# Second addition of signs issued behind the next thresholds on GpSimd, in a fused top-32 attention and mixture-of-experts kernel

## The chip, the cores and the metric

One NeuronCore of a Trainium2 chip runs the whole program. The metric is the device time of one execution in microseconds (us); the number before is the median of three executions.

## What is computed

Attention over 8 batches and 8 heads, 576 tokens, head size 64, where each query keeps only its 32 largest scores; then a layer of 8 experts, of which each token uses the one with the largest gate.

```python
scores = scale * np.matmul(q, k.transpose(0, 1, 3, 2))
kth = np.partition(scores, -top_k, axis=-1)[..., -top_k:-top_k + 1]
mask = scores >= kth                       # top_k = 32
scores = np.where(mask, scores, -1000000000.0)
attn = softmax(scores); attn_out = np.matmul(attn, v)
...
expert_idx = np.argmax(x @ w_gate, axis=1)
h = np.maximum(x[mask] @ w1[e], 0.0); out[mask] = gate_w[mask, None] * (h @ w2[e])
```

(`softmax` stands for the reference's shift, exponential and division.)

## The kernel before, in words

The attention is worked off in 144 groups. A group is two blocks of 128 query rows, each with its 576 scores, so one tile of 128 x 2 x 576 numbers, called `sb` in the profile (seven of them rotate). What happens to group g, by function, line and engine:

- `scores` and `scores_left` (L371, L389): TensorE multiplies into PSUM (tiles `ps`, `px`), ScalarE copies to `sb` (L386, L406), and SyncE issues the DMA that keeps the raw scores in DRAM (`sc`, L423).
- `topk` (L434): VectorE finds the 32nd largest score of every row. Its list `one` has 24 MAX8 instructions over pieces of 48 scores (L1079), `two` merges them (L1086), and `three_`, five instructions, ends it: one reduction of L450, two reductions of L1082 on VectorE, and two small GpSimd instructions of L1082 that make the thresholds, tile `nb`. `three_` is kept in `delayed` and issued in the next step, between that step's MAX8 instructions.
- `softmax(g, us, i)` (L488), once for each of the two blocks i: ScalarE compares the scores with the threshold (activation Sign with `nb` as its bias, L494) and writes signs to the tile `sg` of that block (there is one `sg` for i = 0 and one for i = 1, written in every step); GpSimd adds the signs into the scores in place (L495). The signs are coded so that scores under the threshold vanish in the exponential.
- `transp` (L497): TensorE transposes the masked scores into PSUM (`tt`, nine instructions, L501); `exps` (L503): ScalarE exponentiates them (L505); `av` (L508): TensorE multiplies with the values (`px`, L515).

The order is written out by hand: no scheduler moves instructions, and each engine executes its own list in the order of the Python calls. The main loop (L1059) does, in step t, in this order: `exps` of group t-4, `softmax` of group t-2 for block 0, what jobs have left for TensorE, `scores` of group t+3, `softmax` of t-2 for block 1, `av` of t-5, `scores_left` of t+3, `transp` of t-3, ScalarE's part of jobs; then the 24 MAX8 of group t with the `delayed` thresholds of group t-1 between the first nine of them, then `two` of group t (with one small GpSimd instruction, tile `nbt`) and VectorE's part of jobs; then the jobs' GpSimd part. Jobs are pieces of other work (`advance`, L944): preparing q and k, sums and scaled output rows of finished heads (tiles `sums`, `xm`, `lp`), the repair of rows with ties (`r_...`), and routing of tokens to experts (`table`). So the thresholds that `softmax` of group t-1 will need in step t+1 are computed by VectorE early in step t, and GpSimd finishes them in step t behind both additions of group t-2.

After the last group the expert layer runs: TensorE multiplies by the experts' weights (L1264, L1279), which are split into two parts (L1009 to L1012).

Of the kernel before, what the change touches and what calls it, by code (L numbers as in the profile page):

```python
# [14 lines left out]
OP = mybir.AluOpType  # L15
# [15 lines left out]
LAG = 2  # L31
# [24 lines left out]
def attention_moe(ctx, tc, q, k, v, w_gate, w1, w2, out):  # L56
    nc = tc.nc
# [121 lines left out]
    SG = []  # L179
    for i in range(2):  # L180
        t = consts.tile([128, S], BF, name=f"sg{i}")
# [3 lines left out]
    def upper(t):  # L185
        return t.bitcast(I8).rearrange("p (n b) -> p n b", b=2)[:, :, 1]
# [25 lines left out]
    for b in range(2):  # L212
        for p in range(HP):
            for h in range(2):
# [4 lines left out]
                a = attr[:, t0:t0 + 2 * MAIN - 1:2, :]  # L219
# [4 lines left out]
                a = attr[h * LEFT:(h + 1) * LEFT, tl_, :]  # L224
# [8 lines left out]
    for i in range(3):  # L233
        t = work.tile([128, 2, KW], F32, name=f"qk{i}", bufs=1)
# [30 lines left out]
    for i in range(NV):  # L265
        t = jobs.tile([128, 2, VW], F32, name=f"rv{i}", bufs=1)
# [4 lines left out]
    VV, SB, EX, ET, XT, SCD, SCP = {}, {}, [], {}, {}, {}, {}  # L271
# [22 lines left out]
    def flush(queue):  # L294
        while queue:
            queue.pop(0)()

    def load_v(n):
        b, hf = divmod(n, H // 4)
        rv = VV[n] = VB[n % NV]  # L300
        VV.pop(n - NV, None)
        w = MAIN * D
        for g in range(2):
            hs = slice(4 * hf + 2 * g, 4 * hf + 2 * g + 2)
            both = bass.AP(rv.tensor, rv[:, g].offset, [list(rv.ap[0]), [w + 4 * D, 2], [1, w]])
            nc.sync.dma_start(both, v[b, hs, 0:M, :].rearrange("h (p i) d -> p h (i d)", p=128))
            for i in range(2):
                o = w + (1 - i) * D
                nc.sync.dma_start(rv[i * LEFT:(i + 1) * LEFT, g, o:o + 4 * D].rearrange("p (h x) -> p h x", h=2)[:, :, 0:D],
                                  v[b, hs, M:S, :].rearrange("h p d -> p h d"))  # L310
# [48 lines left out]
    def grp(t):  # L359
        if t < 0 or t >= steps:  # L360
            return []
        n, s = divmod(t, NT)
        p = 2 * n
        if s < MAIN:
            return [p * NT + s, p * NT + MAIN + s]
        if s == MAIN:
            return [p * NT + 2 * MAIN, (p + 1) * NT + 2 * MAIN]
        s -= MAIN + 1
        return [(p + 1) * NT + s, (p + 1) * NT + MAIN + s]

    def scores(slot):  # L371

        if not slot:
            return
        EX.append(pair())
        for n, u in enumerate(slot):
            SB[u] = EX[-1][:, n]
            p, j = divmod(u, NT)
            assert p in READY
            h, i = divmod(j, MAIN)  # L380
            w = slice(2 * LEFT + i * 128, 2 * LEFT + (i + 1) * 128) if h < 2 else slice(0, 2 * LEFT)
            r = slice(h * D, (h + 1) * D) if h < 2 else slice(0, 128)
            qk = QK[p % 3][r]
            nc.tensor.matmul(MAINS[:, n], qk[:, 0, w], qk[:, 1, 2 * LEFT:], start=True, stop=True)  # L384

        nc.scalar.activation(bass.AP(EX[-1].tensor, EX[-1].offset, [list(EX[-1].ap[0]), [S + LEFT, 2], [1, M]]), MAINS,  # L386
                             AF.Copy)
# [100 lines left out]
    def softmax(t, us, i):  # L488
        b, lt = divmod(t, 2 * NT)
        if lt == 0 and i == 0:  # L490
            if b % 2 == 0:
                CNT[b // 2] = jobs.tile([128, 2, NLT], F32, name="cnt")
        nb, u = NB[t], us[i]
        nc.scalar.activation(upper(SG[i]), SB[u], AF.Sign, bias=nb[:, i, 1:2], accum_out=CNT[b // 2][:, b % 2, 2 * lt + i:2 * lt + i + 1])  # L494
        nc.gpsimd.tensor_tensor(SB[u], SB[u], SG[i], op=OP.add)  # L495

    def transp(t):  # L497
        x = EX[t].rearrange("p a s -> p (a s)")
        tt = three.rearrange("p (c q) -> p c q", c=NB9)
        for c in range(NB9):  # L500
            nc.tensor.transpose(tt[:, c], x[:, c * 128:(c + 1) * 128], ident)  # L501

    def exps(t):  # L503
        ET[t] = work.tile([128, NB9, 128], F32, name="et")
        nc.scalar.activation(ET[t], three.rearrange("p (c q) -> p c q", c=NB9), AF.Exp,  # L505
                             bias=shift(t // (2 * NT))[:, 0:1], scale=0.125)

    def av(t, us):  # L508
        et = ET[t]

        def one(px, p, h, n, q):
            rv = VV[p // 2]
            for kb in range(KB):
                blk = MAIN if kb == MAIN else n * (MAIN + 1) + kb
                yield lambda kb=kb, blk=blk: nc.tensor.matmul(  # L515
                    px[h * 64:(h + 1) * 64], block(rv, p % 2, kb if kb < MAIN else MAIN + n, h), et[:, blk, q],
                    start=(kb == 0), stop=(kb == KB - 1))

        def both(a, b):
            for x, y in zip(a, b):  # L520
                x()
                y()

        p, j = divmod(us[0], NT)
        if j < 2 * MAIN:
            px = PX[:, (j % 2) * 128:(j % 2 + 1) * 128]
            both(*(one(px, p, h, h, slice(0, 128)) for h in range(2)))
            if p not in XT:
                XT[p] = jobs.tile([128, S], F32, name="xt", bufs=4)
            if j % 2:  # L530
                act(nc.scalar.activation, XT[p][:, (j - 1) * 128:(j + 1) * 128], PX, AF.Copy)
        else:
            XT[p + 1] = jobs.tile([128, S], F32, name="xt", bufs=4)
            for n in range(2):
                px = PX[:, n * LEFT:(n + 1) * LEFT]
                both(*(one(px, p + n, h, n, slice(h * LEFT, (h + 1) * LEFT)) for h in range(2)))
                act(nc.scalar.activation, XT[p + n][:, 512:S], px, AF.Copy)
# [401 lines left out]
    def start(lane, job, due=0):  # L939
        lanes[lane].append((due, job))  # L940
        if len(lanes[lane]) == 1:
            wants[lane] = next(job)
# [36 lines left out]
    def prep(p):  # L979
        if p < P:  # L980
            start(f"prep{p % 2}", j_prep(p))
# [76 lines left out]
    delayed = []  # L1058
    for t in range(steps + LAG + TD + 4):  # L1059
        n, s = divmod(t, NT)  # L1060
        if grp(t - LAG - TD - 1):
            exps(t - LAG - TD - 1)
        if grp(t - LAG):
            softmax(t - LAG, grp(t - LAG), 0)
        flush(pq)
        scores(grp(t + LA))
        if grp(t - LAG):
            softmax(t - LAG, grp(t - LAG), 1)
        if grp(t - LAG - TD - 2):
            av(t - LAG - TD - 2, grp(t - LAG - TD - 2))  # L1070
        scores_left(grp(t + LA))
        if grp(t - LAG - TD):
            transp(t - LAG - TD)
        flush(lq)
        flush(aq)
        one, two, last = topk(t, grp(t)) if grp(t) else ([], [], [])
        for m in range(max(len(one), 9)):
            if m < len(one):
                one[m][0](*one[m][1])  # L1079
            if m % 2 == 0 and delayed:  # L1080
                f, a = delayed.pop(0)
                f(*a)  # L1082
        delayed = last
        mine, dq[:] = dq[:], []
        for f, a in two:
            f(*a)  # L1086
            if mine:
                mine.pop(0)()
        flush(mine)
        m = t - LAG + 1  # L1090
        if m > 0 and m % (4 * NT) == 0:
            start("find", j_find(m // (4 * NT) - 1), t + DUE['find'])
            start("redo", j_redo(m // (4 * NT) - 1), t + DUE['redo'])
        if m > 2 * NT and m % (2 * NT) == PEAK and m // (2 * NT) + 1 < B:
            start("peak", j_peak(m // (2 * NT) - 1), t - 9)
        m = t - LAG + 1
        if 0 <= m < steps and m % NT == NT - 1:
            start("sums", j_sums(m // NT), t + DUE['sums'])
        if t < steps:
            advance(s=s)  # L1100
            flush(gq)
        else:
            for _ in range(TAIL if t < steps + TADV else 0):
                advance(None)
                for queue in (gq, pq, lq, aq, dq):
                    flush(queue)
        for at, job, a in AHEAD if first else ():
            if t - steps == at:
                job(*a)
        m = t - LAG - TD - 3  # L1110
        if m >= 0 and m % NT == NT - 1:
            start("rows", j_rows(m // NT), t + DUE['rows'])
        if s == PA:
            prep(2 * n + 4)
        if s == PB:
            prep(2 * n + 3)
        if s == LQ and n + 2 < NQ:
            load_qk(n + 2)
        if s == LV and 0 < n < NQ:
            load_v(n)  # L1120
# [497 lines left out]
```

## Time and profile before

| what | value |
|---|---|
| median of 3 executions | 1284.72 us (1282.67 to 1284.81) |
| the profiled execution, its own time | 1284.31 us |
| span of the profiled execution, first to last instruction | 1282.4 us |
| busy: TensorE, VectorE, ScalarE, GpSimd | 91%, 75%, 63%, 66% of the span |
| first and last Sign instruction of the attention | 32.3 and 757.8 us after the start |
| mean granted TensorE clock | 0.976 |

In the rows of the profile PE is TensorE, PEld its loading of weights, DVE VectorE, ACT ScalarE, POOL GpSimd, SP SyncE. A row of a group of instructions gives line, engine, operation, tile written and tiles read, shape, count, busy time and mean duration, and behind the last bar the idle time of the engine before them with what ended it. In the waits view the engine and line that waited stand first, then the one waited for, total time, number of waits and the longest. The first part, up to about 760 us, is the attention, the rest the expert layer.

### The profile page before, as it was taken

How to read it: one execution, taken by the hardware profiler on the slowest of the kernel's cores; microseconds unless marked ns; L12 is line 12 of the kernel's file. 1: busy time of each engine (PE TensorE's matmuls, PEld its weight loads, DVE VectorE, ACT ScalarE, POOL GpSimd, SP SyncE). 2: the span in 40 equal slices, each digit the busy share in tenths (PEclk: the TensorE clock that was granted, in tenths of full speed). 3: DMA queues.
4: the chain of work that ended last, by engine and by line, in shares of the span. 5: the costliest groups of instructions: out<-in, count | busy, mean ns of one | idle time of the engine just before them, and what ended most of it. 6: DMA issues, size and time to landing. Idle time of an engine off the chain costs nothing.

```text
span 1282.4 us, 32272 instructions
## 1 busy us (share of the span) xinstructions
PE 1164.8 (91%) x9589; PEld 914.1 (71%) x9589; DVE 957.6 (75%) x6480; ACT 813.8 (63%) x1649; POOL 843.3 (66%) x1370
## 2 busy tenths in 40 slices
PE   5889998999898889987989858999899999999997
PEld 2566666666665666665666657889799998988996
DVE  6989999999999898998999946636573333323763
ACT  3999999998898798986998842433232323233442
POOL 5677778886889886887886876565643324244654
PEclk8999999999999899997999988999999999999999
DMA  6645665665565465656464525645544333357773
GB/s 172 197 158 170 199 208 164 178 199 157 167 181 174 158 188 162 192 150 171 145 187 144 173 72 166 197 131 181 144 147 144 115 109 119 101 165 218 220 210 102
DMA packets 269081, 209.50 MB, mean 163 GB/s; under 512 B 134407, under 2 KB 212400, under 8 KB 268896
## 3 DMA queue, kind: packets, MB, share of 16 engines
q1 hardware_dynamic: 259216, 185.69, 48.2%
q0 software_dynamic: 8448, 21.37, 5.3%
q8 instruction: 78, 1.28, 0.5%
q14 instruction: 107, 0.88, 0.2%
q10 hardware_dynamic: 1232, 0.30, 0.1%
HBM read 101.10 MB, written 107.33 MB: 163 GB/s over the span
## 4 chain that ended last, share of the span: by engine, by line
PE 40%; DVE 30%; POOL 11%; ACT 9%; issue 7%; DMA 1%; SPq 1%; POOLq 0%; ACTq 0%; DVEq 0%
DVE vq L1079 15%; PE ph L1264 15%; PE y L1279 14%; DVE vq L1086 6%; PE pt L280 4%; ACT sg L494 3%; POOL sb L495 3%; ACT sb L386 2%; PE ps L384 2%; POOL wl L1012 2%; PE px L515 2%; POOL table L899 1%; PE tt L501 1%; ACT qk L280 1%; PE mt L1244 1%
## 5 line engine op out<-in xcount | busy, mean ns | idle before, releaser
L495 POOL TENSOR_TENSOR sb<-sb,sg 128x576 f32<-128x576 f32 x288 | 366.9, 1282 | 126.1 <-ACT sg L494 120.0
L1079 DVE MAX8 vq<-sb 128x8 f32<-128x48 f32 x3456 | 430.1, 200 | 4.4 <-ACT sb L386 4.1
L1012 POOL TENSOR_TENSOR wl<-r,wh 128x512 fp32r<-128x512 f32 x102 | 132.1, 1296 | 212.1 <-DVE wh L1011 206.9
L494 ACT ACTIVATE sg<-sb,nb 128x576 int8<-128x576 f32 x288 | 223.0, 774 | 65.2 <-POOL nb L1082 64.5
L515 PEld LDWEIGHTS px<-et,rv 128*64 128x64 f32 x3200 | 161.4, 139 | 129.0 <-ACT xt L280 61.3
L515 PE MATMUL px<-et,rv 128*64 128x128 f32 (+1 forms) x3200 | 194.8, 271 | 19.0 <-ACT xt L280 12.9
L384 PE MATMUL ps<-qk 64*128 64x512 f32 (+1 forms) x576 | 182.4, 660 | 19.5 <-ACT sb L386 13.8
L1265 ACT ACTIVATE hh<-ph 128x320 fp32r<-128x320 f32 (+2 forms) x128 | 56.2, 439 | 225.1 <-PE ph L1264 210.1
L501 PE MATMUL tt<-turner,sb 128*128 128x128 f32 x1296 | 175.3, 281 | 12.0 <-ACT et L505 9.1
L505 ACT ACTIVATE et<-tt,shifts 128x1152 f32<-128x1152 f32 x144 | 176.3, 1224 | 0.8 <-PE tt L501 0.8
L501 PEld LDWEIGHTS tt<-turner,sb 128*128 128x128 f32 x1296 | 140.4, 141 | 36.2 <-issue 21.8
L386 ACT ACTIVATE sb<-ps 128x1024 f32<-128x1024 f32 x144 | 145.6, 1011 | 31.9 <-PE ps L384 31.8
L1264 PE MATMUL ph<-xh,wh 128*128 128x320 f32 (+2 forms) x504 | 161.0, 320 | 0.0
L1266 DVE SCALAR_TENSOR_TENSOR hl<-ph,hh 128x320 fp32r<-128x320 f32 (+2 forms) x128 | 62.6, 489 | 127.0 <-ACT hh L1265 107.5
L1264 PE MATMUL ph<-xl,wh 128*128 128x320 f32 (+2 forms) x504 | 156.4, 310 | 0.0
L1264 PE MATMUL ph<-xh,wl 128*128 128x320 f32 (+2 forms) x504 | 156.4, 310 | 0.0
L1279 PE MATMUL y<-wh,hl 128*128 128x512 f32 x316 | 125.3, 396 | 4.2 <-DVE hl L1266 4.2
L1012 DVE TENSOR_TENSOR wl<-r,wh 128x512 fp32r<-128x512 f32 x102 | 91.1, 893 | 51.0 <-ACT wh L1009 43.2
L1279 PE MATMUL y<-wh,hh 128*128 128x512 f32 x316 | 125.0, 396 | 0.0
L1279 PE MATMUL y<-wl,hh 128*128 128x512 f32 x316 | 125.0, 395 | 0.0
L1086 DVE MAX8 vq<-vq 128x8 f32<-128x49 f32 (+1 forms) x576 | 120.3, 209 | 0.0
L1264 PEld LDWEIGHTS ph<-xh,wh 128*128 128x128 f32 x504 | 95.2, 189 | 5.8 <-issue 1.8
(288 smaller groups left out, 2046.5 us busy)
## 6 DMA issues: line engine op xcount, KB each, us to landing
r<-in_moe_w_dram SPq DMA_DIRECT2D x204, 256.0 KB
sc<-sb SPq DMA_DIRECT2D x128, 288.0 KB
sc<-sb SPq DMA_DIRECT2D x128, 256.0 KB
rv<-in_v_dram SPq DMA_DIRECT2D x32, 256.0 KB
xs<-xm SPq DMA_DIRECT2D x16, 512.0 KB
rq<-in_q_dram SPq DMA_DIRECT2D x60, 128.0 KB
rk<-in_k_dram SPq DMA_DIRECT2D x60, 128.0 KB
sc<-sb SPq DMA_DIRECT2D x32, 144.0 KB
```

Of the source, the lines that this page charges most:

```text
L384: nc.tensor.matmul(MAINS[:, n], qk[:, 0, w], qk[:, 1, 2 * LEFT:], start=True, stop=True)
L386: nc.scalar.activation(bass.AP(EX[-1].tensor, EX[-1].offset, [list(EX[-1].ap[0]), [S + LEFT, 2], [1, M]]), MAINS, AF.Copy)
L494: nc.scalar.activation(upper(SG[i]), SB[u], AF.Sign, bias=nb[:, i, 1:2], accum_out=CNT[b // 2][:, b % 2, 2 * lt + i:2 * lt + i + 1])
L495: nc.gpsimd.tensor_tensor(SB[u], SB[u], SG[i], op=OP.add)
L501: nc.tensor.transpose(tt[:, c], x[:, c * 128:(c + 1) * 128], ident)
L505: nc.scalar.activation(ET[t], three.rearrange("p (c q) -> p c q", c=NB9), AF.Exp, bias=shift(t // (2 * NT))[:, 0:1], scale=0.125)
L515: yield lambda kb=kb, blk=blk: nc.tensor.matmul(px[h * 64:(h + 1) * 64], block(rv, p % 2, kb if kb < MAIN else MAIN + n, h), et[:, blk, q] ...
L1012: (nc.gpsimd if i else nc.vector).tensor_tensor(lo, r, hi, op=OP.subtract)
L1079: one[m][0](*one[m][1])
L1086: f(*a)
L1264: nc.tensor.matmul(ph, a[:, c, :], x[:, c, s], start=(m == 0), stop=(m == len(seq) - 1))
L1279: nc.tensor.matmul(PY[u, t], a[:, s], x, start=(f == 0 and m == 0), stop=(f == FC - 1 and m == 2))
```

## The change

`softmax` no longer issues GpSimd's addition; it hands it back as a function. For block 0 the main loop calls it at once, as before. For block 1 it is kept, and called after the loop that issues the MAX8 instructions and the delayed thresholds.

```diff
         nc.scalar.activation(upper(SG[i]), SB[u], AF.Sign, bias=nb[:, i, 1:2], accum_out=CNT[b // 2][:, b % 2, 2 * lt + i:2 * lt + i + 1])
-        nc.gpsimd.tensor_tensor(SB[u], SB[u], SG[i], op=OP.add)
+        return lambda: nc.gpsimd.tensor_tensor(SB[u], SB[u], SG[i], op=OP.add)
...
         if grp(t - LAG):
-            softmax(t - LAG, grp(t - LAG), 0)
+            softmax(t - LAG, grp(t - LAG), 0)()
         flush(pq)
         scores(grp(t + LA))
-        if grp(t - LAG):
-            softmax(t - LAG, grp(t - LAG), 1)
+        add = softmax(t - LAG, grp(t - LAG), 1) if grp(t - LAG) else lambda: None
...
             if m % 2 == 0 and delayed:
                 f, a = delayed.pop(0)
                 f(*a)
+        while delayed:
+            f, a = delayed.pop(0)
+            f(*a)
+        add()
         delayed = last
```

The new `while` finds nothing left to do, since 24 MAX8 leave room for all five delayed instructions. The lists of TensorE and VectorE stay as they were, word for word; so do SyncE's apart from the numbers of tiles. GpSimd's list changes in every step. These are two steps in the middle of the attention, before; `sg_149` are the signs of block 0, `sg_151` those of block 1, L1082 makes the thresholds, L1086 is the small instruction of `two`, L280 a job:

```order
L495 TENSOR_TENSOR sb<-sb,sg_149 128x576 [waits DMAHW7_49,DMAHW0_49,Activation_49]
L495 TENSOR_TENSOR sb<-sb,sg_151 128x576 [waits DMAHW1_49,Activation_49]
L1082 TENSOR_TENSOR nb_285<-vq_309,factors 128x4 [waits DVE_49]
L1082 TENSOR_TENSOR nb_285<-nb_285,nbt_281 128x2 [waits Pool_49]
L1086 TENSOR_SCALAR nbt_281<-vq_309,shifts 128x2 [waits DVE_49]
L280 TENSOR_TENSOR sums<-sums,less 128x18
```

And the same place after the change, where the thresholds have the line L1081 and the small instruction L1089:

```order
L495 TENSOR_TENSOR sb<-sb,sg_149 128x576 [waits DMAHW7_49,DMAHW0_49,Activation_49]
L1081 TENSOR_TENSOR nb_285<-vq_309,factors 128x4 [waits DVE_49]
L1081 TENSOR_TENSOR nb_285<-nb_285,nbt_281 128x2 [waits Pool_49]
L495 TENSOR_TENSOR sb<-sb,sg_151 128x576 [waits DMAHW1_49,Activation_49]
L1089 TENSOR_SCALAR nbt_281<-vq_309,shifts 128x2 [waits DVE_49]
L280 TENSOR_TENSOR sums<-sums,less 128x18
```

The second addition has moved behind the two threshold instructions and stays ahead of everything else. ScalarE's list keeps its order, but one wait in it changes. Before, one step of it early in the attention (L494 are the two Signs, L386 and L406 the copies of scores, L505 the exponential):

```order
L494 ACTIVATE sg_149,cnt<-sb,nb_282 128x576 [waits Activation_49,Pool_49]
L386 ACTIVATE sb<-ps 128x2x512 [waits DVE_49,PE_49]
L494 ACTIVATE sg_151,cnt<-sb,nb_282 128x576 [waits Activation_49]
L406 ACTIVATE sb<-px 128x128 [waits PE_49]
L505 ACTIVATE et<-tt,shifts 128x1152 [waits PE_49]
```

And after:

```order
L494 ACTIVATE sg_149,cnt<-sb,nb_282 128x576 [waits Activation_49,Pool_49]
L386 ACTIVATE sb<-ps 128x2x512 [waits DVE_49,PE_49]
L494 ACTIVATE sg_151,cnt<-sb,nb_282 128x576 [waits Pool_49]
L406 ACTIVATE sb<-px 128x128 [waits PE_49]
L505 ACTIVATE et<-tt,shifts 128x1152 [waits PE_49]
```

The second Sign overwrites the signs that the second addition of the group before has read. Before, the first Sign's wait for the thresholds covered that, since the thresholds stood behind that addition; now the second Sign waits for GpSimd itself.

## The prediction

> **What bounds the kernel now.** I read the page's busy times and groups first, then busy time by stretches of the attention, then who waits for whom there, and last one step on ScalarE and GpSimd in the timeline. The page: busy times, the group of the additions and that of the Signs.
>
> ```profile
> PE 1164.8 (91%) x9589; PEld 914.1 (71%) x9589; DVE 957.6 (75%) x6480; ACT 813.8 (63%) x1649; POOL 843.3 (66%) x1370
> ...
> L495 POOL TENSOR_TENSOR sb<-sb,sg 128x576 f32<-128x576 f32 x288 | 366.9, 1282 | 126.1 <-ACT sg L494 120.0
> ...
> L494 ACT ACTIVATE sg<-sb,nb 128x576 int8<-128x576 f32 x288 | 223.0, 774 | 65.2 <-POOL nb L1082 64.5
> ```
>
> The additions take 1.28 us each, GpSimd waits 120.0 us for Signs, and ScalarE waits 64.5 us for thresholds: two engines that wait for each other in turn. The shares of the page are means over two different halves, so I cut the attention out and split it. The columns are PE, PEld, DVE, ACT, POOL busy, then the granted TensorE clock.
>
> ```profile
> core 0: us, PE busy (x) PEld busy (x) DVE busy (x) ACT busy (x) POOL busy (x), PEclk, DMA share, GB/s
> 60.00:740.00 680.00, 614.66 (x6237) 439.07 (x6236) 645.95 (x5506) 596.26 (x1214) 535.08 (x885) 0.98 0.57 173
> ...
> 60.00:200.00 140.00, 128.93 (x1330) 92.46 (x1331) 129.80 (x1175) 130.95 (x263) 107.21 (x171) 1.00 0.60 183
> 200.00:370.00 170.00, 156.26 (x1609) 111.32 (x1609) 166.61 (x1388) 152.02 (x313) 131.62 (x220) 1.00 0.59 179
> 370.00:437.00 67.00, 56.49 (x560) 40.14 (x556) 62.84 (x542) 53.51 (x112) 60.08 (x101) 0.95 0.53 163
> 437.00:560.00 123.00, 115.31 (x1173) 82.50 (x1174) 116.50 (x961) 111.89 (x231) 93.76 (x158) 1.00 0.60 183
> 560.00:600.00 40.00, 29.27 (x260) 20.16 (x259) 36.53 (x311) 26.72 (x54) 35.15 (x60) 0.90 0.47 124
> 600.00:740.00 140.00, 128.40 (x1316) 92.50 (x1315) 133.66 (x1137) 121.17 (x246) 107.27 (x180) 0.98 0.54 168
> ```
>
> In 60 to 740 us VectorE is busy 95% (645.95 of 680), TensorE 90%, ScalarE 88%, GpSimd 79%. So VectorE is nearly full and has 34.05 us of idle time to give; nothing that leaves its work alone can take more than that out of this part. The waits in the same 680 us:
>
> ```profile
> POOL sb L495 <- ACT sg L494: 95.9, 142, 4.5
> ACT sg L494 <- POOL nb L1082: 60.8, 83, 3.5
> PEld px L515 <- ACT xt L280: 57.2, 55, 1.9
> ...
> DVE xm L280 <- PE pt L280: 18.0, 11, 3.6
> ...
> PEld tt L501 <- POOL nb L1082: 5.1, 30, 0.2
> ...
> PEld tt L501 <- POOL sb L495: 4.7, 9, 1.4
> ...
> PE tt L501 <- POOL sb L495: 2.9, 5, 1.1
> ```
>
> VectorE's largest wait is for TensorE (18.0 us, the scaled output rows), and TensorE's largest for ScalarE. There is no wait of GpSimd's thresholds for VectorE, although they read what VectorE computes. A count tells why. Instructions of L1082 begun by 119.7 us:
>
> ```profile
> L1082 DVE TENSOR_REDUCE vq<-vq 128x18 f32<-128x36 f32 (+1 forms) x44 | 7.7, 174 | 0.0
> L1082 POOL TENSOR_TENSOR nb<-vq,factors 128x4 f32<-128x4 f32 x19 | 3.8, 199 | 0.1
> ```
>
> VectorE has two such reductions a group, so 22 groups are reduced when GpSimd has made the thresholds of 19. VectorE runs ahead, until a job makes it wait for TensorE. What it waits for is the train of ScalarE, GpSimd and TensorE behind it. One step of that train without jobs, on ScalarE and then on GpSimd:
>
> ```profile
> 205.63 0.78 ACT L494 ACTIVATE sg<-sb,nb 128x576 int8<-128x576 f32 x1
> ...
> 206.39 1.02 ACT L386 ACTIVATE sb<-ps 128x1024 f32<-128x1024 f32 x1
> 207.29 0.78 ACT L494 ACTIVATE sg<-sb,nb 128x576 int8<-128x576 f32 x1
> ...
> 208.21 1.24 ACT L505 ACTIVATE et<-tt,shifts 128x1152 f32<-128x1152 f32 x1
> 210.00 0.78 ACT L494 ACTIVATE sg<-sb,nb 128x576 int8<-128x576 f32 x1 [0.55 <-POOL nb L1082]
> ```
>
> ```profile
> 206.58 1.28 POOL L495 TENSOR_TENSOR sb<-sb,sg 128x576 f32<-128x576 f32 x1 [0.83 <-ACT sg L494]
> 208.24 1.29 POOL L495 TENSOR_TENSOR sb<-sb,sg 128x576 f32<-128x576 f32 x1 [0.38 <-ACT sg L494]
> 209.48 0.20 POOL L1082 TENSOR_TENSOR nb<-vq,factors 128x4 f32<-128x4 f32 x1
> 209.76 0.20 POOL L1082 TENSOR_TENSOR nb<-nb,nbt 128x2 f32<-128x2 f32 x1
> 210.06 0.31 POOL L1086 TENSOR_SCALAR nbt<-vq,shifts 128x2 f32<-128x2 f32 x1
> ```
>
> This is a closed ring: first Sign at 205.63, copy, second Sign at 207.29, second addition 208.24 to 209.53, thresholds until 209.96, next first Sign at 210.00. The step takes 4.37 us, of which ScalarE idles 0.55. The first addition had ended at 207.86, so the thresholds stood 1.6 us behind an addition that has nothing to do with them.
>
> **The change part by part.** *The thresholds move ahead of the second addition.* In the step above they could start at 207.86 and end 0.48 us later (209.48 to 209.96), at 208.34, instead of 209.96. ScalarE's exponential runs from 208.21 to about 209.45, so the next first Sign could start at 209.45 and the 0.55 us are gone: the ring now closes over the first Sign, the first addition and the thresholds, 208.34 - 205.63 = 2.7 us, far under the step. What is late next in such a step is ScalarE itself, 4.37 - 0.55 = 3.82 us, and in the mean VectorE.
>
> What goes in all is the 60.8 us of waits, if nothing replaced them; but the train gains time for the end only as long as VectorE has idle time to give. By the six stretches, ScalarE's wait for thresholds is
>
> ```profile
> ACT sg L494 <- POOL nb L1082: 9.2, 21, 0.9
> ...
> ACT sg L494 <- POOL nb L1082: 12.9, 18, 3.4
> ...
> ACT sg L494 <- POOL nb L1082: 11.1, 11, 2.4
> ...
> ACT sg L494 <- POOL nb L1082: 6.1, 11, 1.2
> ...
> ACT sg L494 <- POOL nb L1082: 11.0, 6, 3.5
> ...
> ACT sg L494 <- POOL nb L1082: 10.5, 16, 1.4
> ```
>
> and VectorE's idle time, length minus busy, is 10.2, 3.4, 4.2, 6.5, 3.5 and 6.3 us. In the third and fifth stretch GpSimd itself is full (60.08 of 67, 35.15 of 40), so little can go there; its idle time of 6.9 and 4.9 us is still above VectorE's. The smaller of wait and VectorE's idle is 9.2 + 3.4 + 4.2 + 6.1 + 3.5 + 6.3 = 32.7 us. That is the upper bound from this part, for it asks that VectorE never wait at all. The lower bound is nothing: ScalarE and TensorE are both busy 92% and more in the first stretch, and an engine that no longer waits for GpSimd may wait for the other instead (the 57.2 us in which TensorE waits for a copy on ScalarE show how closely they are coupled). I take half, 16.4 us, because I know no row that is nearer to one end.
>
> Outside these 680 us the Signs wait another 64.5 - 60.8 = 3.7 us, at the start and in the last steps, where VectorE is not the bound; half of it, 1.8 us.
>
> *The second addition moves behind the thresholds.* It starts later by at most their 0.48 us; in the step above it would wait for its Sign until 208.24 anyway, and thresholds until 208.34, so 0.10 us. Who waits for it: the transposes of the next step on TensorE, 44 times now (30 + 9 + 5 waits, 12.7 us). Cover is the time from the end of the addition to the moment when TensorE comes to the transposes; where there is none, each costs 0.48 us. Between 0 and 44 x 0.48 = 21 us; I take 0, because 30 of the 44 are waits of 0.2 us at most, which look like the handover alone.
>
> *New wait in front of the second addition.* The thresholds need VectorE's reductions, and with them the second addition, the small instruction and the jobs behind them on GpSimd. VectorE is three groups ahead at 119.7 us, so it costs nothing there. If the train catches up, the thresholds wait, but then VectorE sets the pace, and it doesn't wait for the train: the cost ends where the gain does. 0.
>
> *New wait in front of the second Sign.* It stands behind the second addition of the group before, which now ends about 1.29 us after the thresholds. ScalarE needs 207.29 - 205.63 = 1.66 us from the first Sign to the second, by the Sign and the copy. So 0.3 us of cover are left; 0, and without the copy (the last three groups) up to 0.5 us each.
>
> No DMA is moved, and SyncE's queue isn't touched. The sum: 16.4 + 1.8 = 18.2 us less than the profiled execution's 1284.31, so 1266.1 us. The median of the runs shown is 0.4 us above that execution, which I leave out: 1266 us.
>
> **The rivals.** *More: the train stops holding VectorE up at all.* All 32.7 us and the 3.7 us: 1284.3 - 36.4 = 1248 us. For it speaks that the ring falls to 2.7 us, against it that four engines at 79% to 95% seldom mesh without waits. A variant of it runs over the clock. The third and fifth stretch, where the Signs wait longest, have a granted clock of 0.95 and 0.90, and the first has 1.00; 0.05 x 67 + 0.10 x 40 = 7.4 us of TensorE's time are lost there. If those waits were what lowered it, the gain would be 18.2 + 7.4 = 25.6 us, 1258.7 us. [...] Chance of over 26 us gained: 0.14.
>
> *The gain is swallowed.* ScalarE's idle time moves from the Sign to the exponential or the copies, where it waits for TensorE, and the train keeps its pace; VectorE goes on waiting for TensorE. For it speak TensorE's 614.66 busy us of 680, against it that TensorE's own largest wait is for ScalarE. At most a fifth of the 32.7 us remains: 1278 to 1284 us, with no change as its centre. Chance 0.19, of which 0.11 within 0.2%, about what a measurement of this kernel can tell from no change.
>
> *Slower: the transposes pay.* TensorE takes its list in order, and the transposes of group g stand between one step's products and the next step's scores. Where GpSimd sets the pace (third and fifth stretch, and wherever additions follow each other without a gap), the second addition ends 0.48 us later, the transposes start later, and so do the next scores. At the 14 waits for additions (9 + 5) that is 6.7 us, 1291 us with no gain elsewhere; at all 44 it is 21 us, 1305 us. It decides if TensorE comes to its transposes less than 0.48 us after the addition in most steps. For it speaks the step above, where the addition ends at 209.53 and 30 releases are credited to the thresholds right behind it; against it that the train as a whole starts earlier. [...] Chance 0.11.
>
> **How the numbers follow.** The forecast, a gain of 8 to 26 us (a quarter to four fifths of 32.7), has 0.56; more 0.14, swallowed 0.19, slower 0.11. Faster by over 0.2%, 2.6 us: 0.56 + 0.14 + 0.08 = 0.78. Within: 0.11. Slower: 0.11. The range leaves out some 0.03 below 1250 (the bound of 32.7 us and a little) and 0.15 above 1284 (slower, and part of no change).
>
> **What would show it.** Right: the Signs' wait for thresholds falls from 64.5 us to under 20; in steps without jobs the first Signs come closer than 4.37 us; VectorE's wait for TensorE at `xm` falls under 9 us and its busy share in the attention rises over 97%; the last Sign starts about 18 us before 757.8 us; the expert layer keeps its length. Wrong: waits of the second Sign for additions, or of TensorE's transposes for additions well over the present 7.6 us; or an unchanged `xm` wait, with ScalarE's idle time now at the exponential.

## The result, and the profile after

| kernel | median of four executions, us (lowest to highest) | ratio to the kernel before, 95% interval |
|---|---|---|
| before | 1284.57 (1282.67 to 1284.81) | |
| changed | 1251.39 (1248.73 to 1254.67) | 0.9746 [0.9721, 0.9771] |

The change makes the kernel 33 us faster. The profiled execution took 1251.12 us with a span of 1249.3. Its page, with the busy times, the two groups that were shown of before, and two groups that wait more than they did (12.0 and 31.9 us then):

```profile
PE 1161.7 (93%) x9589; PEld 914.7 (73%) x9589; DVE 952.8 (76%) x6480; ACT 806.3 (65%) x1649; POOL 837.4 (67%) x1370
...
L495 POOL TENSOR_TENSOR sb<-sb,sg 128x576 f32<-128x576 f32 x288 | 369.0, 1281 | 91.6 <-ACT sg L494 88.9
...
L494 ACT ACTIVATE sg<-sb,nb 128x576 int8<-128x576 f32 x288 | 229.2, 796 | 22.9 <-POOL nb L1081 21.5
...
L501 PE MATMUL tt<-turner,sb 128*128 128x128 f32 x1296 | 179.3, 282 | 20.6 <-POOL sb L495 15.3
...
L386 ACT ACTIVATE sb<-ps 128x1024 f32<-128x1024 f32 x144 | 149.5, 1038 | 41.0 <-PE ps L384 40.3
```

The Signs wait 21.5 us for thresholds instead of 64.5, and the additions are as long as they were. Some waiting has moved: TensorE's transposes now wait 15.3 us for additions (in the waits of before, 2.9), and ScalarE's copy of scores idles 41.0 us, 40.3 of them for TensorE (31.8 before). What decides, as the runs with added work will show, is VectorE. Here is the stretch from 60 us to the last MAX8 of the attention, first before (it starts at 740.5 us), then after (709.5 us); the third busy time is VectorE's:

```profile
60.00:740.50 680.50, 614.88 (x6237) 439.07 (x6236) 646.45 (x5511) 596.76 (x1215) 535.58 (x886) 0.98 0.57 174
```

```profile
60.00:709.50 649.50, 607.74 (x6233) 436.31 (x6233) 640.57 (x5507) 591.53 (x1215) 533.63 (x889) 0.99 0.59 182
```

Length minus busy, VectorE's idle time has fallen from 34.05 to 8.93 us, and its busy time by 5.9. So the last MAX8 comes 31.0 us earlier. The last Sign (757.8 and 722.1 us) then follows 12.6 us later instead of 17.3, another 4.7 us, and from there to the end it takes 527.2 us instead of 524.6. 31.0 + 4.7 - 2.6 = 33.1 us, the difference of the spans. From 200 to 300 us VectorE had no idle time before (busy 100.00 us of 100), and there the change gains nearly nothing: the MAX8 that started at 204 us are 10.7 us earlier now, those of 302 us 11.8.

The waits after, from 60 to 710 us:

```profile
POOL sb L495 <- ACT sg L494: 68.4, 70, 4.1
...
PEld px L515 <- ACT xt L280: 35.8, 39, 1.9
...
ACT sg L494 <- POOL nb L1081: 21.5, 16, 3.3
PEld tt L501 <- POOL sb L495: 20.8, 26, 1.8
...
PE tt L501 <- POOL sb L495: 14.7, 19, 1.6
...
DVE xm L280 <- PE pt L280: 4.1, 7, 1.0
```

VectorE's wait for TensorE at the output rows has gone from 18.0 to 4.1 us: TensorE has the products ready in time. One step in the middle shows the opened ring, ScalarE first, then GpSimd:

```profile
196.02 0.80 ACT L494 ACTIVATE sg<-sb,nb 128x576 int8<-128x576 f32 x1
...
196.78 1.04 ACT L386 ACTIVATE sb<-ps 128x1024 f32<-128x1024 f32 x1
197.69 0.80 ACT L494 ACTIVATE sg<-sb,nb 128x576 int8<-128x576 f32 x1
...
198.92 1.27 ACT L505 ACTIVATE et<-tt,shifts 128x1152 f32<-128x1152 f32 x1
200.02 0.83 ACT L494 ACTIVATE sg<-sb,nb 128x576 int8<-128x576 f32 x1
```

```profile
196.99 1.29 POOL L495 TENSOR_TENSOR sb<-sb,sg 128x576 f32<-128x576 f32 x1 [0.35 <-ACT sg L494]
198.23 0.20 POOL L1081 TENSOR_TENSOR nb<-vq,factors 128x4 f32<-128x4 f32 x1
198.51 0.20 POOL L1081 TENSOR_TENSOR nb<-nb,nbt 128x2 f32<-128x2 f32 x1
198.66 1.28 POOL L495 TENSOR_TENSOR sb<-sb,sg 128x576 f32<-128x576 f32 x1
```

The thresholds end at 198.71, 1.3 us before the next Sign begins, and ScalarE goes from the exponential to the Sign without a wait. The step takes 4.00 us, though a copy for a job (`xt`) is in it.

### The profile page after: what moved, and what is told of

Same layout as the page of the kernel before. It is cut to its first block, busy times and chain, and to the rows that moved or that the text cites. A ratio compares the mean times of both kernels' runs of the same rounds, so it can differ in the third digit from the quotient of the medians.

```text
span 1249.3 us, 32272 instructions
## 1 busy us (share of the span) xinstructions
PE 1161.7 (93%) x9589; PEld 914.7 (73%) x9589; DVE 952.8 (76%) x6480; ACT 806.3 (65%) x1649; POOL 837.4 (67%) x1370
## 3 DMA queue, kind: packets, MB, share of 16 engines
q8 instruction: 78, 1.28, 0.5%
## 4 chain that ended last, share of the span: by engine, by line
PE 54%; DVE 24%; POOL 7%; ACT 6%; issue 6%; DMA 2%; SPq 1%; DVEq 0%; POOLq 0%; ACTq 0%
PE ph L1267 15%; PE y L1282 14%; DVE vq L1078 12%; PE px L515 6%; PE ps L384 6%; PE pt L280 5%; PE tt L501 5%; DVE vq L1089 5%; POOL wl L1012 2%; ACT sg L494 2%; ACT sb L386 1%; POOL table L899 1%; PE mt L1247 1%; ACT et L505 1%; PE px L399 1%
## 5 line engine op out<-in xcount | busy, mean ns | idle before, releaser
L494 ACT ACTIVATE sg<-sb,nb 128x576 int8<-128x576 f32 x288 | 229.2, 796 | 22.9 <-POOL nb L1081 21.5
L515 PE MATMUL px<-et,rv 128*64 128x128 f32 (+1 forms) x3200 | 192.1, 269 | 9.0 <-ACT xt L280 5.9
L501 PE MATMUL tt<-turner,sb 128*128 128x128 f32 x1296 | 179.3, 282 | 20.6 <-POOL sb L495 15.3
L505 ACT ACTIVATE et<-tt,shifts 128x1152 f32<-128x1152 f32 x144 | 178.0, 1236 | 1.7 <-PE tt L501 1.4
L386 ACT ACTIVATE sb<-ps 128x1024 f32<-128x1024 f32 x144 | 149.5, 1038 | 41.0 <-PE ps L384 40.3
L1089 DVE MAX8 vq<-vq 128x8 f32<-128x49 f32 (+1 forms) x576 | 122.6, 214 | 0.0
```

The source lines that it names most:

```text
L515: yield lambda kb=kb, blk=blk: nc.tensor.matmul(px[h * 64:(h + 1) * 64], block(rv, p % 2, kb if kb < MAIN else MAIN + n, h), et[:, blk, q] ...
```

## The experiments

Theory A: before, the ring of Sign, copy, Sign, addition and thresholds set the pace of ScalarE, GpSimd and TensorE; in steps without jobs it was longer than VectorE's own step, so that they fell behind and VectorE had to wait for them; the change shortens the ring, and VectorE becomes the limit. That VectorE's own step lies between is seen in the trace of before, in the runs of MAX8 of two steps that follow each other:

```profile
191.89 2.18 DVE L1079 MAX8 vq<-sb 128x8 f32<-128x48 f32 x19
...
196.03 2.19 DVE L1079 MAX8 vq<-sb 128x8 f32<-128x48 f32 x19
```

4.14 us from one to the next, while the ring of before took 4.37. Both lengths are common. Of the 125 steps of before that start from 60 to 700 us, 49 have their first Signs 4.35 to 4.40 us apart, and none is shorter; 43 have their first MAX8 4.14 to 4.20 us apart, and none is shorter. After the change, 45 of 133 steps have first Signs less than 4.14 us apart, many of them 3.68. The main rival B: the place of the second addition behind a threshold instruction, or the second Sign's new wait, brings the gain. Ratios are to the kernel before, run on the same chip.

**Only the subtraction behind the addition, `subtract_behind`.** The changed kernel, but the last threshold instruction is behind the second addition:

```diff
-            if m % 2 == 0 and delayed:
+            if m % 2 == 0 and len(delayed) > 1:
                 f, a = delayed.pop(0)
                 f(*a)
+        add()
         while delayed:
             f, a = delayed.pop(0)
             f(*a)
-        add()
```

> The changed kernel, but only the first of the two threshold instructions (the multiplication) stands ahead of the second addition; the second (the subtraction of nbt), which ends the thresholds, is issued behind it. Theory A (the gain comes from thresholds that are finished before the second addition): the ring of first Sign, copy, second Sign, second addition, thresholds is closed again and one step without jobs lasts 4.3 to 4.4 us; the time goes back to that of the kernel before, 1280 to 1290 us. Rival B (the gain comes from the second addition starting later, or from the second Sign now waiting for GpSimd itself): the addition still starts 0.2 us later and most of the gain stays, 1250 to 1262 us.

Measured: 1262.7 us, 0.9844 [0.9826, 0.9862]. Neither number came: 21 us of the gain are there, with the ring closed. My expectation had the length of the ring wrong. ScalarE and GpSimd in one step of this kernel:

```profile
202.88 0.78 ACT L494 ACTIVATE sg<-sb,nb 128x576 int8<-128x576 f32 x1 [0.27 <-POOL nb L1085]
...
206.96 0.78 ACT L494 ACTIVATE sg<-sb,nb 128x576 int8<-128x576 f32 x1
```

```profile
203.83 1.29 POOL L495 TENSOR_TENSOR sb<-sb,sg 128x576 f32<-128x576 f32 x1 [0.58 <-ACT sg L494]
205.08 0.20 POOL L1081 TENSOR_TENSOR nb<-vq,factors 128x4 f32<-128x4 f32 x1
205.49 1.28 POOL L495 TENSOR_TENSOR sb<-sb,sg 128x576 f32<-128x576 f32 x1 [0.22 <-ACT sg L494]
206.73 0.19 POOL L1085 TENSOR_TENSOR nb<-nb,nbt 128x2 f32<-128x2 f32 x1
```

The multiplication now fits into the time in which GpSimd waits for the second Sign anyway, so the ring is 206.96 - 202.88 = 4.08 us long instead of 4.37. That is under VectorE's 4.14. So 0.29 us, which bring the ring under 4.14, are worth 21 of the 33 us; or else it is B, since the addition does stand behind one threshold instruction. `signs_first` below tells that apart.

**Half of the addition ahead, `half_ahead`.** The function that `softmax` hands back takes the columns to add:

```diff
+        add(slice(0, HALF))
...
-        add()
+        add(slice(HALF, S))
```

> The changed kernel with the second addition cut in two: columns 0 to 287 ahead of the thresholds, where the whole addition stood before, columns 288 to 575 behind them. The ring gets about 0.65 us of addition back of 1.28, so a step without jobs could close in about 4.37 - 0.65 = 3.7 us. Theory A with VectorE as the limit (its steps take longer than 3.7 us): most of the gain of 33 us stays, 1250 to 1262 us; some of that for GpSimd's extra instruction. Rival C (each us of the addition on the ring costs alike): half of the gain is lost, 1265 to 1271 us.

Measured: 1259.16 us, 0.9823 [0.9794, 0.9852]. Some 24 of the 33 us stay, as the first expectation has it. Rival C, for which each us of addition on the ring costs alike, asked for 1265 us or more, and the slowest execution took 1263.6.

**The Signs side by side, `signs_first`.** The kernel before, GpSimd's list untouched; only ScalarE's order changes, and with it the ring:

```diff
             softmax(t - LAG, grp(t - LAG), 0)
+            softmax(t - LAG, grp(t - LAG), 1)
         flush(pq)
         scores(grp(t + LA))
-        if grp(t - LAG):
-            softmax(t - LAG, grp(t - LAG), 1)
```

> The kernel before with GpSimd's list unchanged (both additions ahead of the thresholds), but ScalarE issues the second Sign right behind the first one, ahead of the copy of scores. The ring then runs over the first Sign, both additions without a gap, and the thresholds: 0.95 us from the start of the first Sign to the start of the addition (205.63 to 206.58 in the trace of before), 2.56 us of additions, 0.48 of thresholds and 0.04, 4.03 us instead of 4.37. Theory A in its form for the ring (what counts is whether the ring is shorter than VectorE's mean step): much of the gain without moving any addition, 1255 to 1270 us, as the kernel with only the subtraction behind had 1262.7 with a ring of 4.08 us. Rival B (what counts is that the second addition stands behind a threshold instruction): no gain, 1280 us or more. Against A speaks that the copy, and with it the next scores on TensorE, come 0.78 us later.

Measured: 1261.36 us, 0.9827 [0.9809, 0.9845]. For these 23 us B isn't needed: GpSimd's list is as before, and the first Sign's wait for the thresholds still covers the second Sign. The ring, on ScalarE and on GpSimd:

```profile
199.56 0.78 ACT L494 ACTIVATE sg<-sb,nb 128x576 int8<-128x576 f32 x1
...
200.33 0.76 ACT L494 ACTIVATE sg<-sb,nb 128x576 int8<-128x576 f32 x1
...
203.57 0.80 ACT L494 ACTIVATE sg<-sb,nb 128x576 int8<-128x576 f32 x1
```

```profile
200.51 2.53 POOL L495 TENSOR_TENSOR sb<-sb,sg 128x576 f32<-128x576 f32 x2 [0.58 <-ACT sg L494]
203.00 0.20 POOL L1081 TENSOR_TENSOR nb<-vq,factors 128x4 f32<-128x4 f32 x1
203.27 0.19 POOL L1081 TENSOR_TENSOR nb<-nb,nbt 128x2 f32<-128x2 f32 x1
```

203.57 - 199.56 = 4.01 us: both additions and the thresholds behind them, and still under 4.14. The stretch to the last MAX8 in these three kernels, in the order of the text (`subtract_behind`, `half_ahead`, `signs_first`):

```profile
60.00:719.60 659.60, 612.70 (x6228) 439.89 (x6228) 638.99 (x5505) 594.62 (x1213) 529.38 (x886) 0.98 0.59 179
```

```profile
60.00:716.70 656.70, 610.05 (x6225) 434.61 (x6226) 639.24 (x5499) 590.95 (x1208) 553.43 (x1019) 0.99 0.59 180
```

```profile
60.00:716.60 656.60, 607.75 (x6237) 439.88 (x6233) 640.22 (x5502) 592.08 (x1209) 531.68 (x887) 0.98 0.59 180
```

VectorE's idle time is 20.6, 17.5 and 16.4 us, between 34.05 before and 8.93 after, and the times (1262.7, 1259.2, 1261.4) lie in between as well. So a ring under 4.14 us doesn't bring everything: the closest first Signs in these three are 4.06, 3.80 and 3.92 us apart, in the changed kernel many are 3.68. Shorter steps would let the engines behind VectorE catch up sooner after a step with jobs; that this is the reason for the last 10 us is an argument, and no run shows it by itself.

**More work for VectorE, `max_load_after` and `max_load_before`.** Two MAX8 a step that nobody needs, in the changed kernel and in the kernel before:

```diff
                 one[m][0](*one[m][1])
+                if m in (11, 17):
+                    nc.vector.max(spare, ident[:, 0:48])
```

> The changed kernel with two more MAX8 of 48 columns in every step on VectorE, over a constant, whose results nobody reads; the nineteen that follow each other in a step take 0.11 us each, so this is 144 x 0.22 = 32 us of work for VectorE. Theory A (VectorE now sets the pace of the attention, with 9 us of idle time left between 60 and 710 us): slower by 22 to 34 us, 1273 to 1285 us. Rival D (TensorE and ScalarE set the pace now, each handing waits to the other): slower by under 10 us, under 1262 us.

> The kernel before with the same two additional MAX8 a step on VectorE, 32 us of work. Theory A (before, the train of ScalarE, GpSimd and TensorE set the pace and VectorE had 34 us of idle time between 60 and 740 us): a good part goes into the idle time, slower by 3 to 16 us, 1288 to 1301 us. Rival E (VectorE set the pace before as well, since it was busy 95%): slower by 25 to 34 us, 1310 to 1319 us.

Measured: 1270.75 us after, 0.9915 [0.9888, 0.9942], 19 us more than the changed kernel; 1286.93 us before, 1.0025 [1.0013, 1.0038], 3.4 us more. The stretch to the last MAX8, after and then before:

```profile
60.00:730.80 670.80, 615.80 (x6235) 440.12 (x6233) 669.24 (x5791) 594.48 (x1219) 535.27 (x890) 0.98 0.58 176
```

```profile
60.00:743.40 683.40, 615.43 (x6250) 439.84 (x6246) 673.23 (x5786) 599.76 (x1221) 537.77 (x892) 0.99 0.57 173
```

The same work, some 28 us of busy time (669.24 - 640.57 and 673.23 - 646.45), costs 19 us in one kernel and 3.4 in the other. After, VectorE's idle time goes from 8.9 to 1.6 us and the rest prolongs the attention; before, it goes from 34.05 to 10.2 and nearly all is swallowed. VectorE's first MAX8 of two steps that follow each other, in `max_load_before`:

```profile
193.34 0.20 DVE L1080 MAX8 vq<-sb 128x8 f32<-128x48 f32 x1
...
197.71 0.20 DVE L1080 MAX8 vq<-sb 128x8 f32<-128x48 f32 x1
```

Its step without jobs has become 4.37 us long, as long as the ring, so the two now run level; that is why the work fits in. This is the plainest evidence for A: busy 95%, VectorE wasn't the limit before; busy 98.6%, it is now. The expectation for `max_load_after` missed by 2 us at its lower end: the added work is 28.7 us in this stretch, where the expectation reckoned with 32, and 7.4 of it went into idle time.

**Both additions behind, `both_behind`.**

```diff
-            softmax(t - LAG, grp(t - LAG), 0)()
+            add0 = softmax(t - LAG, grp(t - LAG), 0)
...
+        if grp(t - LAG):
+            add0()
         add()
```

> Both additions of a step stand behind the thresholds on GpSimd: thresholds, first addition, second addition. The thresholds then wait for VectorE alone, and the second addition is no longer later than its own Sign and the first addition make it. Theory A with VectorE as the limit (9 us of its idle time left in the attention): no more than 9 us to gain over the changed kernel; 1243 to 1252 us. Rival D (the additions' place holds the train up, TensorE now waits 35 us in its transposes for the second addition): a larger gain, under 1243 us. Rival F (the first Sign now has to wait for the first addition of the group before, which is on a new ring): slower than the changed kernel, over 1255 us.

Measured: 1251.29 us, 0.9746 [0.9724, 0.9767], as the changed kernel. Its waits from 60 to 710 us:

```profile
PEld tt L501 <- POOL sb L495: 23.5, 35, 2.2
ACT sg L494 <- POOL sb L495: 22.1, 18, 3.3
PE tt L501 <- POOL sb L495: 14.8, 23, 2.0
```

The Signs no longer wait for thresholds at all, they wait as long for additions; the transposes wait 38.3 us for additions, although nothing stands between the two additions any more. Neither D nor F holds: these waits are slack in front of VectorE, and moving them doesn't move the end.

**No wait of the second Sign, `third_sign_tile`.** The second signs take turns in two tiles (the Sign's own line writes to `sg` likewise):

```diff
-    for i in range(2):
+    for i in range(3):
         t = consts.tile([128, S], BF, name=f"sg{i}")
...
+        sg = SG[i * (1 + t % 2)]
-        return lambda: nc.gpsimd.tensor_tensor(SB[u], SB[u], SG[i], op=OP.add)
+        return lambda: nc.gpsimd.tensor_tensor(SB[u], SB[u], sg, op=OP.add)
```

> The changed kernel with two tiles for the second signs that take turns, so that the second Sign no longer waits for the second addition of the group just before, but for that of two groups before. It prices the wait that the change added. Forecast by the trace of the changed kernel, where Signs wait 1.3 us for additions: no difference that can be told, 1248 to 1253 us. If the wait were hidden in others: faster by 3 us and more.

Measured: 1249.77 us, 0.9728 [0.9705, 0.975]; the changed kernel's 0.9746 lies in that interval. The new wait costs nothing that can be told.

**Signs of both blocks in turn, both additions behind, `both_behind_four`.** As the two before, together, with two tiles for each block:

```diff
+        sg = SG[i + 2 * (t % 2)]
...
+        if grp(t - LAG):
+            add0()
         add()
```

> Both additions behind the thresholds, and two tiles for the signs of each block that take turns, so that no Sign waits for an addition of the group just before (in the kernel with both behind, Signs wait 22.5 us for additions). Theory A with VectorE as the limit (8 us of its idle time left): at most a few us below the changed kernel, 1243 to 1252 us. Rival D (the Signs' waits still cost one for one): 1225 to 1238 us.

Measured: 1250.88 us, 0.9748 [0.9729, 0.9767]. Half of the Signs' waits are gone (11.2 us are left, for thresholds) and nothing is gained.

**VectorE's jobs a step later, `rows_last_later`.** The kernel before, with

```diff
+        yield need(slack=1)
         yield need(dve=1.0)
         done(2)
```

> The kernel before, in which VectorE scales the last third of a group of output rows (the xm of 128x256, on which it waits most for TensorE) one step later, so that TensorE has its products ready. Theory A (the train behind VectorE set the pace before, and VectorE's waits only show it): the waits go elsewhere, to the scores or to other jobs, the time stays within 4 us, 1280 to 1287 us. Rival G (VectorE was the bound before, and these 12 us of its waits were the loss): faster by 6 us and more, under 1278 us.

Measured: 1279.15 us, 0.9968 [0.9949, 0.9988], a gain of 5 us, just outside of both expectations. VectorE's waits between 60 and 745 us, the largest:

```profile
DVE skip L280 <- PE pt L280: 6.2, 1, 6.2
DVE xm L280 <- DMA xs<-xm: 5.9, 4, 2.8
DVE less L280 <- ACT vq L280: 5.0, 3, 3.4
...
DVE xm L280 <- PE pt L280: 4.4, 3, 2.1
```

Most of the waiting for TensorE's products has moved to other jobs, as A has it. VectorE's idle time up to the last MAX8 fell only from 34.05 to 29.8 us. That some 5 us are gained shows that A isn't the whole story. VectorE idled only 3.4 us of 170 in the part from 200 to 370 us before, and might have been the limit there; but the gain doesn't lie in that part alone. The first Signs are 1.1 us earlier at 200 us, 3.4 at 370, 4.0 at 600 and 5.9 at the end. Why stays open.

**A faster version, `third_tile_rows_later`, beside the changed kernel, `changed_again`.** The changed kernel with the third tile of signs and the last rows a step later:

```diff
+        sg = SG[i * (1 + t % 2)]
...
+        yield need(slack=1)
         yield need(dve=1.0)
         done(2)
```

> The changed kernel with two tiles for the second signs that take turns, and with VectorE's scaling of the last third of the output rows one step later, as in two runs before. VectorE has 9 us of idle time left in the attention of the changed kernel, 4 of them at these rows. Theory A (VectorE's work is the limit): 1 to 5 us faster than the changed kernel, 1245 to 1250 us. If the step's delay only moves the waits, no difference: 1249 to 1253 us.

> The changed kernel itself, beside the one with two tiles and later rows, on the same chip. 1248 to 1254 us, as before.

Measured: 1246.88 us, 0.9713 [0.97, 0.9727], and 1252.06 us, 0.9748 [0.9732, 0.9763]. The intervals don't overlap; 5 us come on top, about the upper end of the expectation. The later rows weren't tried alone in the changed kernel; the third tile alone gave 0.9728, within the interval of the changed kernel's first measurement ([0.9721, 0.9771]). The trace doesn't show where the 5 us lie: the last MAX8 starts at 709.8 us, in the two traces of the changed kernel at 709.5 and 711.9.

## Why the prediction was right, and where it was off

**The mechanism** was right: the thresholds no longer stand behind the second addition, the step shown takes 4.00 us, and many steps take 3.68, near the 3.82 that the prediction left for ScalarE. 1251 lies in the range, 1.4 us above its lower end, but the forecast was 18 us of gain and 33 were measured. The case that came is the rival called "more", which had a chance of 0.14.

**The step that was off** is the half that was taken of 32.7 us: "I take half, 16.4 us, because I know no row that is nearer to one end." Measured, VectorE's idle time to the last MAX8 fell by 25.1 us, and its busy time by 5.9, together 31.0. The 5.9 are in no term of the sum, which took VectorE's work as fixed; that they came too is luck. The reason given for the half, that an engine which no longer waits for GpSimd may wait for another instead, came true in part: ScalarE's copies of scores wait 40.3 us for TensorE instead of 31.8, and TensorE's transposes wait 35.5 us for additions instead of 7.6, while TensorE's largest wait for ScalarE fell from 57.2 to 35.8. `both_behind` and `both_behind_four` shift such waits, and the time stays. There was a row that was nearer to one end, and the prediction didn't use it: VectorE's own step of 4.14 us. The ring was 4.37 long, so in a step without jobs the engines behind VectorE lost 0.23 us, and with no step under 4.35 us they couldn't catch up what they had lost in steps with jobs. The 49 short steps come to some 10 us of that (49 x 0.2); the rest of the 25.1 would then be the catching up, which no run separates. A ring under 4.14 turns it round, as 4.08 and 4.01 did with two thirds of the gain; the rest came with the still shorter steps of the changed kernel. What the wait on the ring was worth depended here on whether the ring was longer (4.37 us) or shorter (4.08, 4.01) than VectorE's step of 4.14.

**The tail**, half of 3.7 us, 1.8, was 4.7 us to the last Sign, less the 2.6 us from there to the end. These 2.6 say little: in the traces of this document that part takes between 522.5 and 529.7 us, though no edit touches the expert layer.

**The new waits** were priced at nothing. For the second Sign's, `third_sign_tile` shows it. For the second addition's there is no direct test; `both_behind` puts the first addition behind the thresholds as well, and that costs nothing. The second addition keeps its place behind the thresholds: in the step shown of after it starts at 198.66 us, behind the threshold instructions at 198.23 and 198.51, and in both traces all 288 additions and 288 threshold instructions start in the order of GpSimd's list. The sign that was named for the slower rival, transposes that wait well over 7.6 us, did appear, and didn't mean what the prediction said. TensorE comes to its transposes earlier now, and waits there for the same thing; its idle time in the stretch to the last MAX8 fell from 65.6 to 41.8 us.

**The other signs**: the Signs' wait fell to 21.5 us, not quite under 20; VectorE's busy share rose to 98.6%; `xm` waits 4.1 us for TensorE. The last Sign came 35.7 us earlier, not 18. The variant over the clock plays no part that can be seen: the granted clock is 0.976 before and 0.975 after, and up to the last MAX8 0.98 and 0.99. That the waits lowered the clock, no run shows.

## What to carry to other kernels

Compare the length of each ring (a chain that goes through several engines and comes back to its start one step later) with the step of the busiest engine, not with its own engines' busy shares: here engines at 79% and 88% set the pace, and the busiest one, at 95%, only idled 34.05 us of 680.50, a little here and there. While the ring was the longer one, shortening it by 0.29 us, from 4.37 to 4.08, gave back 13.4 of those 34.05 us (`subtract_behind`). Once it was the shorter one, less was left: 21 us of time came with the ring just under VectorE's step of 4.14, and 12 more when the steps of the engines on it became shorter still. Extra work for an engine, in one run, told whether it was the limit: some 28 us of it on VectorE cost 19 us after the change and 3.4 before.

## What the runs showed of the hardware

VectorE's busy time fell by 5.9 us though its work is the same. Half of that, 3.0 us, sits in three copies of the routing jobs; other small instructions of jobs became shorter or longer, a group of them by up to 1.2 us. The copies before and then after (the last two numbers before the idle time are busy us and mean ns):

```profile
L280 DVE COPY hist<-cum 128x8 bf16<-128x8 bf16 x3 | 3.7, 1217 | 0.0
```

```profile
L280 DVE COPY hist<-cum 128x8 bf16<-128x8 bf16 x3 | 0.7, 218 | 0.0
```

A copy of eight numbers a row takes about the length of a GpSimd addition, 1.28 us, in one kernel and 0.2 us in the other. One of the three before, beside two additions:

```profile
353.60 2.59 POOL L495 TENSOR_TENSOR sb<-sb,sg 128x576 f32<-128x576 f32 x2
...
353.67 1.26 DVE L280 COPY hist<-cum 128x8 bf16<-128x8 bf16 x1
```

All six of these copies begin while an addition is under way, and end 0.04 to 0.12 us behind its end: before, the addition had begun 0.05 to 0.19 us earlier, and after, it had 0.07 to 0.22 us left. So a copy that began at the start of an addition took 1.14 to 1.26 us, and one that began close to its end 0.19 to 0.26; why the copies end with the additions, no run here tested. The three copies take 3.7 us in the trace of before, 0.7 in that of after and 0.6 in that of `max_load_after`; so their time, and VectorE's with it, differs by some 3 us among these kernels.
